# The first layer's last ten chunks by Strassen's scheme too, and the seven products chained in two banks

## Chip, cores and metric

One Trainium2 chip, one core. The metric is the device time of one execution in microseconds (us). Engines: PE is TensorE, DVE is VectorE, ACT is ScalarE, POOL is GpSimd, SP is SyncE, whose queue issues all DMAs of this kernel.

## What is computed

Sliding-window attention (4 batches, 8 heads, 576 positions, head size 64, window 64), then two feed-forward layers over 2304 tokens, each 512 to 2048 to 512, in float32:

```python
attn_out = _attn_ref(q, k, v)                      # softmax over the last 64 positions
x = attn_out.transpose(0, 2, 1, 3).reshape(B * S, H * D)     # 2304 x 512
h = x @ w_in;  g = h * np.clip(h + 3.0, 0.0, 6.0) / 6.0;  x = g @ w_out
h = x @ w2_in; g = np.maximum(0.01 * h, h);               out = g @ w2_out
```

## The kernel before

Every float32 operand of the layers is split into a rounded high half and a low half, and each product is three matmuls: high by high, low by high, high by low. `rounded` and `halves` make the halves of 128 x 512 pieces of the weights, on ScalarE and VectorE; the pieces lie in rings of 7 tiles each (`w0h`, `w0l` for the layer's first weights, `w1h`, `w1l` for its second).

**Plain chunks.** In the first layer a chunk is 128 of the 2048 hidden features. For a block of tokens (four of 512 and one of 256) `st_h` makes 12 matmuls into a PSUM bank `h`; ScalarE and VectorE turn that into the halves `gh` and `gl`; `st_y` makes 12 matmuls into the banks `y0` to `y3`. The 16 chunks go in groups of 6, 5 and 5; a group runs over all blocks before the next begins, and its sums go to `xb` in SBUF (copied for the first group, added by VectorE for the later ones). The attention of block b+1 is spread over block b of the first group; its output `xa0` to `xa4` stays in SBUF for all three groups, and is split into `xs0h` to `xs3l` anew in each.

**Quads.** The second layer works by Strassen's scheme (in Winograd's form). A quad is two chunks in one pass of 768 tokens, and a pass has 8 quads, with 3 passes. Inputs and weights are cut in two by two parts, so that 7 products M1 to M7 of 6 matmuls with 384 columns each (line 848) stand for what would be 8. `inputs` makes the seven input operands of a pass (B11, B21, B22 and the differences T1 to T4). A quad's 11 weight pieces come from `convert_quad`, which makes them on ScalarE and VectorE and stores them to DRAM (`kept`), or from `fetch`, which loads them from there. Four quads are converted ahead, during the first layer (`STAGED`), the other four in the first pass. The sums of the products, their activation and the split into halves give four values C11, C12, C21, C22; 12 groups of three 512-column matmuls (line 921) then take them into six PSUM banks, and these groups of one quad are put between the products of the next, as many after each product as `FILL` says. PSUM has eight banks: two `h`, four `y`, two `a`. Products add up in a bank where the scheme allows: M2 upon M1, M3 upon M5; the rest is added by VectorE (`plus`, line 334).

**Order.** Nothing is ordered by hand except the chain of PE's operations in the second layer. Each operation is noted with its possible engines, an assumed duration and what it reads and writes; `Order.run` then plans the whole program, and every engine gets its instructions in one fixed order, SP's queue too. An engine takes its instructions in that order, so one that waits holds up all behind it.

Of the kernel before, what the change touches and what calls it, by code (L numbers as in the profile page):

```python
# [223 lines left out]
def swa_relu6_leaky_kernel(ctx: ExitStack, tc: tile.TileContext, q, k, v, w_in, w_out, w2_in, w2_out, out):  # L224
# [24 lines left out]
    GROUPS = (6, 5, 5)  # L249
# [8 lines left out]
    NQUAD = NF // 2  # L258
    STAGED = 4
# [12 lines left out]
    kept = [dr.tile([11 * P, DM], F32, name=f"kept{i}") for i in range(NQUAD)]  # L272
# [12 lines left out]
    xa = [buf(f"xa{b}", [P, NK * n], F32, 1) for b, (_, n) in enumerate(blocks)]  # L285
# [237 lines left out]

    def block_of(tok):
        for b, (o, n) in enumerate(blocks):
            if o <= tok < o + n:
                return b, tok - o

    def st_V(n, po, then=None, pps=()):
# [34 lines left out]
        for js, bb, o in groups:  # L564
# [3 lines left out]
                lambda bb=bb, o=o, m=m: xa[bb]().rearrange("p (c l) -> p c l", c=NK)[:, :, o:o + m * W].rearrange(  # L568
# [13 lines left out]
    assert f0 == NF  # L582
# [87 lines left out]

    WAYS = {
# [3 lines left out]
    SEQ = (("M1", "B11"), ("M6", "T2"), ("M2", "B21"), ("M7", "T3"), ("M5", "T1"), ("M4", "T4"), ("M3", "B22"))  # L675
    FILL = (0, 4, 0, 4, 0, 4, 0)
    stage = []
    turn7 = 0
# [5 lines left out]
    def fetch(kk, i):  # L684
        got = ring_tiles(kk)
        for j, t in enumerate(got):
            load(P * DM * 4, lambda t=t: t().bitcast(F32), kept[i][j * P:(j + 1) * P, :], [t], [("kept", i, j)])
        return got

    def convert_quad(i, kk=None):  # L690

        if kk is None:
            if not stage:
                stage.append(buf("at", [P, 9 * DM], F32R, 1))
            homes = [(None, stage[0], lambda j=j: stage[0]()[:, j * DM:(j + 1) * DM]) for j in range(9)]
            got = [od.slot("stage", None, None, None, 0, homes) for _ in range(11)]
        else:
            got = ring_tiles(kk)

        def keep(j):  # L700
            store(P * DM * 4, kept[i][j * P:(j + 1) * P, :], lambda: got[j]().bitcast(F32), [got[j]], [("kept", i, j)])

        f = 2 * i
        a1, a1f = rounded(w2_in[f * P:(f + 1) * P, :])
# [3 lines left out]
        a2, a2f = rounded(w2_in[(f + 1) * P:(f + 2) * P, :])  # L708
# [4 lines left out]
        def combo(dst, d, x, xr, y, yr, alu):  # L713
            op(tensor_tensor(256, d, x, y, alu), [*xr, *yr], [dst])

        combo((s12, 0), lambda: s12()[:, L], lambda: a2f()[:, L], [a2], lambda: a2f()[:, R], [a2], ALU.add)
        combo((s12, 1), lambda: s12()[:, R], lambda: s12()[:, L], [(s12, 0)], lambda: a1f()[:, L], [a1], ALU.subtract)
        halves(DM, lambda: s12()[:, 0:DM], [(s12, 0), (s12, 1)], got[2], got[3], got[2], got[3])
        keep(2)
        keep(3)  # L720
        combo((s34, 0), lambda: s34()[:, L], lambda: a1f()[:, L], [a1], lambda: a2f()[:, L], [a2], ALU.subtract)
        combo((s34, 1), lambda: s34()[:, R], lambda: a1f()[:, R], [a1], lambda: s12()[:, R], [(s12, 1)], ALU.subtract)
        halves(DM, lambda: s34()[:, 0:DM], [(s34, 0), (s34, 1)], got[4], got[5], got[4], got[5])
# [4 lines left out]
        op([("SP", 0.62, lambda: nc.sync.dma_start(out=kept[i][6 * P:7 * P, :], in_=got[6]().bitcast(F32)))],  # L728
           [(got[6], 0), (got[6], 1)], [("kept", i, 6)])
# [362 lines left out]
```

## Time and profile before

| | |
|---|---|
| median of 3 runs | 860.62 us (859.61 to 861.33) |
| the profiled execution | 861.6 us, span 859.8 us |
| PE busy | 843.4 us, 98% |
| DVE, ACT, POOL busy | 537.7, 456.3, 42.6 us |
| DMA | 139.84 MB, mean 163 GB/s |
| mean granted clock of PE | 0.995 |

The span runs from the first to the last instruction; the execution's own time is 1.8 us more. Ends of matmuls are modelled and matmuls overlap, so PE's pace is read from the distance between starts.

### The profile page before, as it was taken

What the parts mean: (1) busy time and instruction counts of PE and PEld (TensorE: products, weight loads), DVE (VectorE), ACT (ScalarE), POOL (GpSimd) and SP (SyncE); (2) the same over time, 40 slices, a digit from 0 to 9 for tenths busy, and PEclk for the clock granted to TensorE, in tenths of its full rate; (3) what the DMA queues carried; (4) which work ended last, traced back from release to release, by engine and by line L of the source; (5) the groups of instructions that cost most, each with busy time, mean ns of one, the idle gap of its engine ahead of it and who ended that gap; (6) DMA issues with size and microseconds to landing.
All of it is one profiled execution on the core that took longest, in us unless ns stands there. A gap on an engine that the chain in (4) does not pass through costs nothing.

```text
span 859.8 us, 13915 instructions
## 1 busy us (share of the span) xinstructions
PE 843.4 (98%) x5104; PEld 728.6 (85%) x5104; DVE 537.7 (63%) x1169; ACT 456.3 (53%) x1024; POOL 42.6 (5%) x45
## 2 busy tenths in 40 slices
PE   6799999999999999999999999999999999999998
PEld 4578888888988888988888999889999998899996
DVE  5999865343788887889884548888432336322323
ACT  4889977563675555665643436666432235422322
POOL 2222221210000000000000000000000000000000
PEclk9999999999999999999999999999999999999999
DMA  8856552100235442365421746669855565764501
GB/s 286 266 176 205 173 185 58 31 24 1 74 111 188 154 146 89 103 216 172 144 76 56 276 144 237 221 220 313 311 191 189 163 210 182 241 215 164 192 29 73
DMA packets 71907, 139.84 MB, mean 163 GB/s; under 512 B 7328, under 2 KB 15520, under 8 KB 71840
## 3 DMA queue, kind: packets, MB, share of 16 engines
q1 hardware_dynamic: 71840, 138.97, 48.7%
q8 instruction: 40, 0.66, 0.3%
q14 instruction: 27, 0.22, 0.1%
HBM read 111.15 MB, written 27.79 MB: 162 GB/s over the span
## 4 chain that ended last, share of the span: by engine, by line
PE 96%; DMA 1%; ACT 1%; SPq 1%; DVE 1%; issue 0%; POOL 0%; DVEq 0%; ACTq 0%
PE h L598 23%; PE y L644 23%; PE h L848 21%; PE y L921 15%; PE a L921 8%; PE a L493 2%; PE h L545 1%; PE a L518 1%; DMA at<-in_v_dram 1%; PE a L545 1%; SPq L337 1%; ACT at L441 0%; PE h L518 0%; PE y L493 0%; PE a L480 0%
## 5 line engine op out<-in xcount | busy, mean ns | idle before, releaser
L644 PE MATMUL y<-gh,w1h 128*128 128x512 f32 (+1 forms) x320 | 119.0, 372 | 0.0
L644 PE MATMUL y<-gl,w1h 128*128 128x512 f32 (+1 forms) x320 | 118.0, 369 | 0.0
L644 PE MATMUL y<-gh,w1l 128*128 128x512 f32 (+1 forms) x320 | 117.9, 368 | 0.0
L848 PE MATMUL h<-xa,w0l 128*128 128x384 f32 x360 | 107.5, 336 | 0.0
L848 PE MATMUL h<-xa,w0h 128*128 128x384 f32 x360 | 107.3, 336 | 0.0
L334 DVE TENSOR_TENSOR qt<-h,qt 128x384 f32<-128x384 f32 x72 | 40.1, 557 | 94.2 <-PE h L848 93.1
L921 PE MATMUL y<-w1h,at 128*128 128x512 f32 x288 | 97.2, 391 | 0.0
L617 ACT ACTIVATE r<-h 128x512 f32<-128x512 f32 (+1 forms) x80 | 44.4, 554 | 98.0 <-PE h L598 97.7
L622 DVE SCALAR_TENSOR_TENSOR r<-r,h 128x512 f32<-128x512 f32 (+1 forms) x80 | 50.6, 632 | 62.4 <-ACT r L617 62.1
L644 PEld LDWEIGHTS y<-gl,w1h 128*128 128x128 f32 x320 | 60.3, 189 | 10.5 <-DVE gl L626 0.4
L644 PEld LDWEIGHTS y<-gh,w1h 128*128 128x128 f32 x320 | 60.3, 189 | 10.1 <-issue 0.3
L644 PEld LDWEIGHTS y<-gh,w1l 128*128 128x128 f32 x320 | 60.4, 189 | 9.6
L848 PEld LDWEIGHTS h<-xa,w0l 128*128 128x128 f32 x360 | 66.5, 188 | 1.8
L848 PEld LDWEIGHTS h<-xa,w0h 128*128 128x128 f32 x360 | 66.4, 188 | 1.8
L825 ACT ACTIVATE qt<-qt 128x384 f32<-128x384 f32 x48 | 25.2, 525 | 74.4 <-DVE qt L334 74.4
L921 PEld LDWEIGHTS y<-w1h,at 128*128 128x128 f32 x288 | 54.1, 188 | 10.6
L626 DVE SCALAR_TENSOR_TENSOR gl<-r,gh 128x512 fp32r<-128x512 f32 (+1 forms) x80 | 51.6, 645 | 14.1 <-ACT gh L319 13.3
L319 ACT ACTIVATE gh<-r 128x512 fp32r<-128x512 f32 (+2 forms) x84 | 48.9, 582 | 17.1 <-DVE r L622 16.8
L357 DVE TENSOR_SCALAR ca<-ca 128x512 uint32<-128x512 uint32 (+1 forms) x128 | 54.5, 434 | 4.8 <-ACT ca L368 4.5
L921 PE MATMUL y<-w1l,at 128*128 128x512 f32 x144 | 56.7, 394 | 0.0
L921 PE MATMUL a<-w1h,at 128*128 128x512 f32 x144 | 50.6, 392 | 0.0
L368 ACT ACTIVATE ca<-st 128x512 f32<-128x512 f32 x64 | 42.5, 669 | 12.5 <-DVE w0l L329 4.0
(206 smaller groups left out, 1828.5 us busy)
## 6 DMA issues: line engine op xcount, KB each, us to landing
w0h<-kept SPq DMA_DIRECT2D x70, 256.0 KB, 3.1
w0l<-kept SPq DMA_DIRECT2D x70, 256.0 KB, 3.1
st<-in_moe_w_in_dram SPq DMA_DIRECT2D x32, 512.0 KB, 3.8
st<-in_moe_w_out_dram SPq DMA_DIRECT2D x32, 512.0 KB, 3.9
kept<-at SPq DMA_DIRECT2D x44, 256.0 KB, 2.3
w1h<-kept SPq DMA_DIRECT2D x40, 256.0 KB, 4.0
w1l<-kept SPq DMA_DIRECT2D x40, 256.0 KB, 4.3
at<-in_v_dram SPq DMA_DIRECT2D x16, 256.0 KB, 3.8
```

Source lines behind the costliest of these rows:

```text
L319: a = act(n, lambda: nc.scalar.activation(out=dst(), in_=src(), func=AF.Copy, scale=scale))
L334: return [dve(n, lambda: nc.vector.tensor_tensor(out=dst(), in0=a(), in1=b(), op=alu))]
L357: return dve(DM, lambda: nc.vector.tensor_scalar(out=dst(), in0=src(), scalar1=s1, scalar2=s2, op0=op0, **({"op1": op1} if op1 else {})), ...
L368: act(DM, lambda: nc.scalar.activation(out=af(), in_=high().bitcast(F32), func=AF.Abs)),
L598: nc.tensor.matmul(ph()[:, 0:n], wt()[:, cs], xt()[:, 0:n], start=(c == 0 and m == 0), stop=(c == NK - 1 and m == 2),)
L617: act(n, lambda: nc.scalar.activation(out=rr(), in_=h(), func=AF.Relu, bias=3.0)),
L622: op([dve(n, lambda: nc.vector.scalar_tensor_tensor(out=rr(), in0=rr(), scalar=6.0, in1=h(), op0=ALU.min, op1=ALU.mult))], [r, ph], [r])
L626: op([dve(n, lambda: nc.vector.scalar_tensor_tensor(out=gl()[:, 0:n], in0=rr(), scalar=1.0 / 6.0, in1=gg().bitcast(F32), op0=ALU.mult, op1 ...
L644: nc.tensor.matmul(y()[:, 0:n], stat()[:, cs], mov()[:, 0:n], start=(first and m == 0), stop=(last and m == 2))
L825: act(HT, lambda: nc.scalar.activation(out=r(), in_=r(), func=AF.Prelu, alpha=0.01)),
L848: nc.tensor.matmul(bk()[:, 0:HT], a, b_(), start=(start and j == 0 and q_ == 0), stop=(j == 1 and q_ == 2), skip_group_check=True,)
L921: nc.tensor.matmul(y(), a()[:, cs], b_(), start=(first and m == 0), stop=(last and m == 2))
```

## The change

The first layer keeps its plain way for the first group of 6 chunks alone. The other ten become five quads, in the same three passes of 768 tokens as the second layer (`QUADS` is 5 and 8). Since the attention output no longer stays in SBUF (`xa` is now a ring of two), `st_h` stores it to DRAM (`xd`), and `inputs` loads the four parts of a pass from there. The first layer's quads have their own activation (`swish`), and their outputs (`outputs0`) go as before into `y0` to `y3` with 512 tokens, and into the two `a` banks with the other 256, to be added to `xb` at a pass's end.

Weights: three of the five quads are converted in the plain part, through the tiles `e0` to `e2`; the other two in the first pass. Four quads of the second layer are converted in the first layer's second and third passes (`AHEAD`), through four tiles of 512 columns (`gh`, `gh`, `gl`, `gl`).

Products, in both layers: the order is now M1, M2, M6, M5, M7, M4, M3. M1, M6, M7 and M4 add up in one `h` bank (`up`), which is copied out to SBUF after M1, M6 and M7; M2 and then M5 with M3 use the other (`side`), and three additions by VectorE join the two. Output groups stand after M6, M7 and, in the first layer, M3.

```diff
-    GROUPS = (6, 5, 5)
+    GROUPS = (6,)
...
-    NQUAD = NF // 2
-    STAGED = 4
+    PLAIN = sum(GROUPS)
+    QUADS = ((NF - PLAIN) // 2, NF // 2)
+    STAGED = (3, 4)
...
-    kept = [dr.tile([11 * P, DM], F32, name=f"kept{i}") for i in range(NQUAD)]
+    xd = dr.tile([P, NK * NT], F32, name="xd").rearrange("p (c l) -> p c l", c=NK)
+    kept = [[dr.tile([11 * P, DM], F32, name=f"kept{j}_{i}") for i in range(n)] for j, n in enumerate(QUADS)]
...
-    xa = [buf(f"xa{b}", [P, NK * n], F32, 1) for b, (_, n) in enumerate(blocks)]
+    xa = [buf("xa", [P, NK * 512]) for _ in blocks]
...
+            store(P * NK * n * 4, xd[:, :, o:o + n], lambda: xblock(b), names, [("xd", b)])
...
-    SEQ = (("M1", "B11"), ("M6", "T2"), ("M2", "B21"), ("M7", "T3"), ("M5", "T1"), ("M4", "T4"), ("M3", "B22"))
-    FILL = (0, 4, 0, 4, 0, 4, 0)
+    SEQ = (("M1", "B11"), ("M2", "B21"), ("M6", "T2"), ("M5", "T1"), ("M7", "T3"), ("M4", "T4"), ("M3", "B22"))
+    FILL = ((0, 0, 8, 0, 4, 0, 4), (0, 0, 6, 0, 6, 0, 0))
+    AHEAD = [(p, i) for p in (1, 2) for i in (0, 2)]
...
-    def convert_quad(i, kk=None):
+    def stage_homes(layer):
...
+            if layer == 0:
+                tiles_ = [buf(f"e{m}", [P, 4 * HT], F32R, 1) for m in range(3)]
+                stage[0] = [(None, t, lambda t=t, j=j: t()[:, j * DM:(j + 1) * DM]) for t in tiles_ for j in range(3)]
+            else:
+                tiles_ = [buf(g, [P, DM], F32R) for g in ("gh", "gh", "gl", "gl")]
+                stage[1] = [(None, t, lambda t=t: t()[:, 0:DM]) for t in tiles_]
+        return stage[layer]
...
+    def convert_quad(layer, i, kk=None):
...
-            if not stage:
-                stage.append(buf("at", [P, 9 * DM], F32R, 1))
-            homes = [(None, stage[0], lambda j=j: stage[0]()[:, j * DM:(j + 1) * DM]) for j in range(9)]
-            got = [od.slot("stage", None, None, None, 0, homes) for _ in range(11)]
+            got = [od.slot(("stage", layer), None, None, None, 0, stage_homes(layer)) for _ in range(11)]
         else:
             got = ring_tiles(kk)
...
-        s12 = buf("kt", [P, 768])
-        s34 = buf("kt", [P, 768])
+        s = buf("st", [P, DM, 2], U32, bufs=3)
...
-    def second_layer():
+    def paired():
...
+        for x, tag in (("B11", "xa"), ("B21", "xa"), ("T2", "e0"), ("T1", "e1"), ("T3", "e2")):
...
+        t = buf("wx", [P, HT], F32, 1)
+        whomes += [(None, t, lambda t=t: t()[:, 0:HT])]
+        gslots = [((grid, j), lambda j=j: grid()[:, j * HT:(j + 1) * HT]) for j in range(12)]
...
+        def inputs(layer, p):
...
+                if layer:
+                    names = [("y1", b, c) for b in over for c in (2 * kh, 2 * kh + 1)]
+                    src[x] = names, lambda: xb[:, 2 * kh:2 * kh + 2, o:o + HT]
+                else:
+                    t = buf("st", [P, DM, 2], U32, bufs=3)
...
+                    load(P * 2 * HT * 4, view, xd[:, 2 * kh:2 * kh + 2, o:o + HT], [t], [("xd", b) for b in over])
...
+        def swish(r, hi, lo):
+            a = work()
+            op([
+                act(HT, lambda: nc.scalar.activation(out=a(), in_=r(), func=AF.Relu, bias=3.0)),
...
+            op([dve(HT, lambda: nc.vector.scalar_tensor_tensor(
+                out=r(), in0=a(), scalar=6.0, in1=r(), op0=ALU.min, op1=ALU.mult
+            ))], [r, a], [r])
+            op(copy(HT, hi[1], r, True, 1.0 / 6.0), [r], [hi[0]])
+            op([dve(HT, lambda: nc.vector.scalar_tensor_tensor(
+                out=lo[1](), in0=r(), scalar=1.0 / 6.0, in1=hi[1]().bitcast(F32), op0=ALU.mult, op1=ALU.subtract
+            ))], [r, hi[0]], [lo[0]])
+
...
+            value = leaky if layer else swish
+            up, side = bank("h", 2), bank("h", 2)
             for pos, (m, x) in enumerate(SEQ):
-                name = {"M1": "X", "M2": "X", "M6": "Y", "M7": "Y", "M4": "Y", "M5": "V", "M3": "V"}[m]
-                if name not in banks2:
-                    banks2[name] = bank("h", 2)
-                bk = banks2[name]
-                product(m, x, bk, m not in ("M2", "M3"))
+                product(m, x, side if m in ("M2", "M5", "M3") else up, m in ("M1", "M2", "M5"))
                 if m == "M1":
-                    wk["s"] = ring("wk", whomes)
-                    op(copy(HT, wk["s"], lambda bk=bk: bk()[:, 0:HT]), [bk], [wk["s"]])
+                    r11 = out_of(up)
+                elif m == "M2":
+                    plus(r11, side)
+                    value(r11, *slots["C11"])
                 elif m == "M6":
-                    plus(wk["s"], bk, wk["s"])
-                elif m == "M2":
-                    g["C11"] = value(ring("wk", whomes), bk)
+                    r12 = out_of(up)
                 elif m == "M7":
-                    wk["u"] = ring("wk", whomes)
-                    plus(wk["u"], bk, wk["s"])
-                elif m == "M5":
-                    r = ring("wk", whomes)
-                    plus(r, bk, wk["u"])
-                    g["C22"] = value(r)
+                    r22 = out_of(up)
+                    plus(r22, side)
+                    value(r22, *slots["C22"])
                 elif m == "M4":
-                    plus(wk["u"], bk, wk["u"])
-                    g["C21"] = value(wk["u"])
-                else:
-                    plus(wk["s"], bk, wk["s"])
-                    g["C12"] = value(wk["s"])
-                for _ in range(FILL[pos]):
+                    if layer:
+                        leaky(work(), *slots["C21"], up)
+                    else:
+                        swish(out_of(up), *slots["C21"])
+                elif m == "M3":
+                    plus(r12, side)
+                    value(r12, *slots["C12"])
+                for _ in range(plan[pos]):
...
-        def values_out(p, i, wt, g):
+        def outputs0(p, i, wt, g):
...
+                def fn():
+                    for m, (a, b_) in enumerate(((hi, gh), (lo, gh), (hi, gl))):
+                        nc.tensor.matmul(
+                            y()[:, d:d + n], a()[:, cs], b_[1]()[:, t0:t0 + n], start=(begins and m == 0),
+                            stop=(last and m1 and m == 2), skip_group_check=(n < 512),
+                        )
...
+            for k, f in enumerate((1, 0)):
+                for n in (512, 256):
+                    for c in range(NK):
+                        todo.append(lambda n=n, f=f, c=c, k=k: part(n, f, c, k == 0, k == 1))
...
+        def outputs1(p, i, wt, g):
...
-            order = [("C11", 0, 0), ("C22", 1, 1), ("C21", 1, 0), ("C12", 0, 1)]
+            order = (("C21", 1, 0), ("C22", 1, 1), ("C11", 0, 0), ("C12", 0, 1))
...
-                                op(copy(DM, z, y), [y], [z])
+                                t = buf("st", [P, DM, 2], U32, bufs=3)
+
                             else:
-                                z = buf(f"xs{c}{'hl'[half]}", [P, DM], F32, 1)
-                                for k in range(2):
-                                    ks = slice(k * 256, (k + 1) * 256)
-                                    src, dst = (lambda ks=ks: y()[:, ks]), (lambda ks=ks: z()[:, ks])
-                                    op([copy(256, dst, src)[k]], [y], [(z, k)])
-                            zs = [z] if p < NPAIR - 1 else [(z, 0), (z, 1)]
+                                t = z = buf(f"xs{c}{'hl'[half]}", [P, DM], F32, 1)
+                            op(copy(DM, z, y), [y], [t])
...
+        for layer in range(2):
+            for p in range(NPAIR):
+                inputs(layer, p)
+                for i in range(QUADS[layer]):
+                    if p == 0 and i >= STAGED[layer]:
+                        wt = convert_quad(layer, i, kk)
+                    else:
+                        wt = fetch(layer, i, kk)
+                    if not layer and (p, i) in AHEAD:
+                        convert_quad(1, AHEAD.index((p, i)))
...
+                    quad(layer, wt, slots, todo, plan)
+                    todo, plan = (outputs1 if layer else outputs0)(p, i, wt, g), FILL[layer]
...
-                if f == GROUPS[0] + GROUPS[1]:
-                    for i in range(STAGED // 2):
-                        convert_quad(i)
                 convert(f)
-                if f == NF - 1:
-                    for i in range(STAGED // 2, STAGED):
-                        convert_quad(i)
+                if f == PLAIN - 1:
+                    for i in range(STAGED[0]):
+                        convert_quad(0, i)
...
-    second_layer()
+    paired()
```

PE, a quad of the first half of the second layer before: M1 (into `h_5823`), then M6 (into `h_5835`), then the first output group. Names are tiles, with the planner's numbers.

```order
L848 MATMUL h_5823<-xa0_4437,w0h_5587 128x384
L848 MATMUL h_5823<-xa0_4437,w0l_5598 128x384
L848 MATMUL h_5823<-xa0_4437,w0h_5587 128x384 x2
L848 MATMUL h_5823<-xa0_4437,w0l_5598 128x384
L848 MATMUL h_5823<-xa0_4437,w0h_5587 128x384
L848 MATMUL h_5835<-xa1_4744,w0h_5626 128x384
L848 MATMUL h_5835<-xa1_4744,w0l_5644 128x384
L848 MATMUL h_5835<-xa1_4744,w0h_5626 128x384 x2
L848 MATMUL h_5835<-xa1_4744,w0l_5644 128x384
L848 MATMUL h_5835<-xa1_4744,w0h_5626 128x384
L921 MATMUL y0_5432<-w1h_5353,at_5369 128x512
```

PE, the start of a first-layer quad in the change: M1 (into `up`, here `h_3392`), M2 (into `side`, `h_3403`), and M6's first matmul.

```order
L887 MATMUL h_3392<-xa_2684,w0h_3152 128x384
L887 MATMUL h_3392<-xa_2684,w0l_3156 128x384
L887 MATMUL h_3392<-xa_2684,w0h_3152 128x384 x2
L887 MATMUL h_3392<-xa_2684,w0l_3156 128x384
L887 MATMUL h_3392<-xa_2684,w0h_3152 128x384
L887 MATMUL h_3403<-xa_2845,w0h_3152 128x384
L887 MATMUL h_3403<-xa_2845,w0l_3156 128x384
L887 MATMUL h_3403<-xa_2845,w0h_3152 128x384 x2
L887 MATMUL h_3403<-xa_2845,w0l_3156 128x384
L887 MATMUL h_3403<-xa_2845,w0h_3152 128x384
L887 MATMUL h_3392<-e0_2786,w0h_3174 128x384
```

M6 has moved from a bank of its own into the bank that M1 has just filled, with one product between the two.

SP, before: DMA issues beside the first layer's later chunks, when quads of the second layer are staged. `st` are weights as they come, `at` holds the staged pieces.

```order
L337 DMA st<-in_moe_w_in_dram 128x1024
L341 DMA kept_70<-at 128x512 x5
L728 DMA kept_70<-at 128x512
L337 DMA st<-in_moe_w_out_dram 128x1024
L341 DMA kept_70<-at 128x512 x2
L337 DMA st<-in_moe_w_in_dram 128x1024
```

SP, in the change: the first layer's second pass. `kept_2_72` and `kept_3_73` are first-layer quads 2 and 3, `kept_0_75` the second layer's quad 0.

```order
L339 DMA w1l<-kept_2_72 128x512
L339 DMA w1h<-kept_3_73 128x512
L339 DMA w0h<-kept_3_73 128x512
L339 DMA w0l<-kept_3_73 128x512
L339 DMA w1l<-kept_3_73 128x512
L343 DMA kept_0_75<-gh 128x512 x2
L339 DMA st<-in_moe_w_out_dram 128x1024 x2
L339 DMA w0h<-kept_3_73 128x512
L339 DMA w0l<-kept_3_73 128x512
L343 DMA kept_0_75<-gl 128x512
L343 DMA kept_0_75<-gh 128x512
```

Where the queue held weights to be converted and stores of staged pieces, it now also holds the fetches that PE needs for its next quads.

## Rows read from the trace of the kernel before

**Rows 1.** The page, busy time of the engines over the whole span.

```profile
PE 843.4 (98%) x5104; PEld 728.6 (85%) x5104; DVE 537.7 (63%) x1169; ACT 456.3 (53%) x1024; POOL 42.6 (5%) x45
```

**Rows 2.** Windows: length, busy us of PE, PEld, DVE, ACT, POOL, clock, DMA.

```profile
0.00:20.00 20.00, 12.60 (x138) 9.19 (x142) 10.26 (x30) 9.36 (x28) 5.12 (x13) 0.96 0.88 282
20.00:40.00 20.00, 15.40 (x225) 11.84 (x217) 17.47 (x40) 16.83 (x41) 5.73 (x5) 0.87 0.85 281
40.00:60.00 20.00, 19.47 (x183) 14.84 (x182) 19.69 (x43) 17.78 (x62) 5.84 (x5) 1.00 0.59 188
240.00:260.00 20.00, 20.00 (x90) 16.57 (x89) 18.31 (x33) 13.29 (x25) 0.00 (x0) 1.00 0.35 123
520.00:540.00 20.00, 20.00 (x101) 17.96 (x100) 17.22 (x37) 12.62 (x25) 0.00 (x0) 1.00 0.58 207
580.00:600.00 20.00, 20.00 (x103) 18.27 (x102) 17.73 (x31) 12.88 (x25) 0.00 (x0) 1.00 0.91 302
600.00:620.00 20.00, 20.00 (x102) 18.05 (x101) 11.07 (x20) 10.12 (x21) 0.00 (x0) 1.00 0.93 324
```

**Rows 3.** The chain that ended last, one quad: start, length, what.

```profile
784.08 3.14 PE h L848 x18
787.22 2.76 PE y L921 x12
789.98 2.10 PE h L848 x12
...
799.72 3.14 PE h L848 x18
```

**Rows 4.** Timeline of PE, first layer, from 512-token to 256-token block: start, length.

```profile
343.56 0.39 PE L644 MATMUL y<-gh,w1h 128*128 128x512 f32 x1
...
344.24 0.28 PE L598 MATMUL h<-xs0h,w0h 128*128 128x256 f32 x1
...
346.75 0.28 PE L598 MATMUL h<-xs0h,w0h 128*128 128x256 f32 x1
```

**Rows 5.** Timeline of all engines around M3, M1 and M6, second layer.

```profile
722.24 0.34 PE L848 MATMUL h<-xs3l,w0l 128*128 128x384 f32 x1
...
722.62 0.56 DVE L334 TENSOR_TENSOR qt<-h,qt 128x384 f32<-128x384 f32 x1 [0.53 <-PE h L848]
...
723.29 0.51 PE L848 MATMUL h<-xa,w0h 128*128 128x384 f32 x2
...
723.66 0.49 ACT L319 ACTIVATE r<-h 128x384 f32<-128x384 f32 x1 [0.69 <-PE h L848]
```

**Rows 6.** Groups by line and shape: count, busy us, mean ns, idle before.

```profile
L329 DVE CUSTOM_DVE_ANT_0 ca<-ca,cr 128x1024 uint16<-128x1024 uint16 x64 | 46.1, 722 | 0.2
L373 DVE SCALAR_TENSOR_TENSOR ca<-st,ca 128x512 uint32<-128x512 uint32 x64 | 45.0, 706 | 0.4
L626 DVE SCALAR_TENSOR_TENSOR gl<-r,gh 128x512 fp32r<-128x512 f32 x64 | 44.9, 702 | 13.0 <-ACT gh L319 12.2
...
L334 DVE TENSOR_TENSOR qt<-h,qt 128x384 f32<-128x384 f32 x72 | 40.1, 557 | 94.2 <-PE h L848 93.1 <-ACT ca L368 0.7
L357 DVE TENSOR_SCALAR ca<-ca 128x512 f32<-128x512 f32 x64 | 27.9, 436 | 4.5 <-ACT ca L368 4.5
...
L660 DVE TENSOR_TENSOR xb<-y,xb 128x512 f32<-128x512 f32 x32 | 21.0, 684 | 3.1 <-PE y L644 3.1
...
L626 DVE SCALAR_TENSOR_TENSOR gl<-r,gh 128x256 fp32r<-128x256 f32 x16 | 6.7, 420 | 1.2 <-ACT gh L319 1.1
...
L329 DVE TENSOR_TENSOR kt<-xb,kt 128x768 f32<-128x768 f32 x6 | 5.7, 953 | 0.1
...
L368 ACT ACTIVATE ca<-st 128x512 f32<-128x512 f32 x64 | 42.5, 669 | 12.5 <-DVE w0l L329 4.0 <-DVE w1l L329 3.1 <-DVE at L329 2.7
...
L825 ACT ACTIVATE qt<-qt 128x384 f32<-128x384 f32 x48 | 25.2, 525 | 74.4 <-DVE qt L334 74.4
...
L319 ACT ACTIVATE qt<-h 128x384 f32<-128x384 f32 x16 | 7.8, 490 | 2.3 <-PE h L848 2.3
```

More of the change, by code (lines that the diff above doesn't have):

```diff
@@ L522, in st_P, with xblock @@
             pts[n].append(pt)
+    def xblock(b):
+        n = blocks[b][1]
+        return xa[b]()[:, 0:NK * n].rearrange("p (c l) -> p c l", c=NK)
     def block_of(tok):
@@ L890, in quad, with part, add @@
                 fill.pop(0)()
-            return g
-        def fetched(wt):
-            return wt[6].whole
         ybanks = {}
-        todo = []
-        def values_out(p, i, wt, g):
+        def outputs0(p, i, wt, g):
+            o = 2 * p * HT
             if i == 0:
+                ybanks.clear()
+                for c in range(NK):
+                    ybanks[c] = bank(f"y{c}")
+                for c in range(0, NK, 2):
+                    ybanks["a", c] = ybanks["a", c + 1] = bank("a", 2)
+            yb = dict(ybanks)
+            first, last = i == 0, i == QUADS[0] - 1
+            todo = []
+            def part(n, f, c, m0, m1):
+                hi, lo = wt[7 + 2 * f], wt[8 + 2 * f]
+                (gh, gl), y = g[f], yb[c] if n == 512 else yb["a", c]
+                d = 0 if n == 512 else (c % 2) * 256
+                t0 = 0 if n == 512 else 512
+                cs = slice(c * P, (c + 1) * P)
+                begins = first and m0 and (n == 512 or c % 2 == 0)
+                def fn():
[4 more added lines that the diff above has]
+                        )
+                op([pe(3 * (0.0132 + n / 2400), fn)], [hi, lo, *gh[0], *gl[0]], [y], chain=True)
+                if last and m1 and (n == 512 or c % 2):
+                    over = [b for b, (s, m) in enumerate(blocks) if s < o + 512 and o < s + m] if n == 512 else \
+                        [b for b, (s, m) in enumerate(blocks) if s < o + 768 and o + 512 < s + m]
+                    cc = (c,) if n == 512 else (c - 1, c)
+                    def add():
+                        if n == 512:
+                            dst, got = xb[:, c, o:o + 512], y()
+                        else:
+                            dst = xb[:, c - 1:c + 1, o + 512:o + 768]
+                            got = y().rearrange("p (c l) -> p c l", c=2)
+                        nc.vector.tensor_tensor(out=dst, in0=got, in1=dst, op=ALU.add)
+                    op([dve(512, add)], [y], [("y1", b, k) for b in over for k in cc])
+            for k, f in enumerate((1, 0)):
+                for n in (512, 256):
+                    for c in range(NK):
+                        todo.append(lambda n=n, f=f, c=c, k=k: part(n, f, c, k == 0, k == 1))
+            return todo
@@ L939, in go @@
+                            op(copy(DM, z, y), [y], [t])
+                            op([("SP", 0.8, lambda: nc.sync.dma_start(out=out[r0:r0 + P, :], in_=z()))], [t],
                                delay=2.0)
[L940 removed]
+                            op([("DMA", P * DM * 4 / 3.6e5, lambda: None)], [t], delay=2.0)
                     todo.append(go)
[L944 to L956 removed]
+            return todo
```

179 lines of the change are left out of this document (98 added, 81 removed).

## The prediction

> **What bounds the kernel now.** I read the page's busy line first, then busy time by stretches, then the chain, then single rows. The busy line gives TensorE (PE) 98% of the span and VectorE (DVE) 63% [rows 1]; a 98% made of pipelined matmuls could still hide waits, so the stretches come next. The first two are the only ones with gaps that matter: PE is busy 12.60 and 15.40 of 20 us, 12.0 us idle, while q, k and v arrive and the softmax runs. Afterwards every stretch shown has PE at 20.00 of 20 and the granted clock at 1.00, whether VectorE is at 18.31 (conversions beside the first layer) or the DMA engines at 0.93 [rows 2]. The chain shows what a saturated PE delivers: a second-layer quad runs from 784.08 to 799.72, 15.64 us, and nothing else stands in it [rows 3]. So time after the start is matmuls times their spacing, and a change is worth what it takes off that sum, less any wait that it opens.
>
> **The spacing.** Three 512-column matmuls of layer one start 0.68 us apart, 0.2267 each, and 21 of 256 columns take 2.51 us, 0.1195 each [rows 4]. In the quad, twelve 512-column ones take 2.76 us, 0.230 each; that leaves (15.64 - 36 x 0.230) / 42 = 0.1752 us for one of 384 columns [rows 3]. At the granted 1.00, the 2.4 GHz level, 512 columns would be 0.2133 us, so each matmul costs about 13 ns beyond its columns, and cutting work into more, shorter matmuls gives part of a saving back. The Trainium skill (TensorE: Matmul & The Clock Gate, Back-to-back issue gap) puts that extra at 2.5 ns; by it the saving below would be 240 x (4 x 0.2158 + 0.1092) - 15 x (42 x 0.1625 + 24 x 0.2158 + 24 x 0.1092) = 14.0 us. The trace does not agree, and the sum goes by the rows.
>
> **What is removed and added on PE.** A plain chunk has 24 matmuls (12 into h, 12 out to y) for each of four blocks of 512 tokens and one of 256: 24 x (4 x 0.2267 + 0.1195) = 24.63 us; ten chunks, 246.3 us. A first-layer quad of the change has 7 products x 6 matmuls of 384 columns and, for two chunks, 24 matmuls of 512 and 24 of 256 into y: 42 x 0.1752 + 24 x 0.2267 + 24 x 0.1195 = 15.67 us; five quads in three passes, 235.0 us. **Gain 11.3 us.** If its 512-column matmuls run at the second layer's 0.230 instead, 236.2 us and a gain of 10.1. The second layer keeps all its matmuls; there I count no gain, since no wait was there to remove.
>
> **Edits costed at nothing, and their cover.** *VectorE.* 50 of 80 chunk steps go, and a first-layer quad brings eight scalar_tensor_tensor of 384 columns (not in the trace; between 0.420 at 256 and 0.702 at 512, I take the middle, 0.561) and three sums at 0.557: 6.2 us. A converted quad is four weight loads of 0.436 + 0.436 + 0.706 + 0.722 and a low half of 0.684 (the fourth without it), four sums at about 0.420 and low halves of 0.684 + 0.684 + 0.420: 14.7 us. New inputs are nine operations of 768 columns at 0.953 and four of 384 at 0.557: 10.8; six sums into xb, 4.1 [rows 6]. A pass has five quads and two conversions: 30.8 + 29.4 + 10.8 + 4.1 = 75.1 us in 78.4 us of PE. The cover is thin, but VectorE at 18.31 of 20 held nothing up [rows 2]. *ScalarE* gets twelve operations of 0.490 to 0.525 a quad, 6.2 us [rows 6], and has the room. *Storing and loading the inputs* (4.7 MB once, then 1.57 MB a pass) and the three quads staged early lie beside the plain chunks, where the DMA share was 0.59 before 60 us and 0.35 at 240 us [rows 2]. If that cover went, a first quad would wait for its inputs, once, for a few us. The start and the tail I leave as they are.
>
> **The sums chained in two banks.** Before, M6 had a bank of its own and M2, the next into M1's bank, stood behind four output groups. Now M6 adds into `up`, so ScalarE must have copied M1's result out while M2 runs. The row for that copy: M1's last matmul starts at 723.29 (the x2 there is this one and M6's first, 0.17 later), the copy starts at 723.66 and takes 0.49, so it is out at 724.15. Six matmuls of M2 in between would put M6 at 723.46 + 6 x 0.1752 = 724.51: 0.36 us to spare, if ScalarE is free [rows 5]. A second-layer quad has two more such places: M4's result must leave `up` during M3, and the sum with M3's must leave `side` during the next M1 (in the first layer four output groups lie between as well). The last is what the trace already has: M3's last matmul starts at 722.24, the sum runs from 722.62 to 723.18, and M6, which needs that bank, starts at 723.46 without a gap, 0.28 later [rows 5]. An operation of 0.5 to 0.67 us that ScalarE has just begun [rows 6] eats this margin and misses it by up to 0.3. What queues behind a late copy is M6, and on ScalarE the activation of C11, which nobody needs for several us. Bounds for the wait per place: 0 (the old place of this kind) and 0.3. With 24 x 3 + 15 x 1 = 87 places I take 1.5 us in all, near the row that shows none; this also stands for the first quads, which have few output groups to put between products.
>
> **DMA.** From the code, a fetched quad is 11 pieces of 256 KB, 2.88 MB, and a converted one 2.10 MB of weights read and 2.88 MB written. Passes two and three of the first layer take ten fetches, four conversions ahead for layer two and two sets of inputs: 28.8 + 19.9 + 3.1 = 51.9 MB in 156.7 us, 331 GB/s. The trace reached 302 and 324 GB/s in neighbouring stretches, at shares of 0.91 and 0.93, that is 332 and 348 at a full share [rows 2]. So these 157 us would run at 95 to 100% of what the rows show, where the old kernel did so for 40. Fetches have slack, because a weight tile of the ring of 14 is refilled for the quad after next. The staged pieces have less: layer two's eleven pass through four tiles (gh, gh, gl, gl), so each write to one waits until its last store has landed, on ScalarE's and VectorE's own queues, with the sums of the products behind it. I take no wait here, since the sum still fits.
>
> **Sum.** Span 859.8 - 11.3 + 1.5 = 850.0. The profiled execution took 861.6 with its 859.8, so it would be 851.8; the median of the runs lies 1.0 below the profiled one, and 860.6 - 11.3 + 1.5 = **850.8 us**.
>
> **Rivals.** *The DMA engines become the bound in passes two and three.* At the stretch's 324 GB/s 51.9 MB take 160.2 us, 3.5 late; at 302, 171.9, 15.2 late; at their mean, 165.8, 9.1 late. That gives 852.8 to 864.5, with 860.6 - 11.3 + 9.1 = 858.4 likeliest. For it: the sum above, the four stage tiles, SyncE's one queue. Against: the ring's slack, and PE at 20.00 beside the share of 0.93. The Trainium skill (DMA: Bandwidth & Descriptors, Bandwidth) speaks for it: it asks for 1 MiB or more a transfer and has 341 GB/s there and 138 at 64 KB, and these are of 256 KB. The trace does not bear that out so far, with 324 GB/s in such pieces.
>
> *The short places cost more than the matmuls save.* It decides at 11.3 / 87 = 0.13 us a place. If ScalarE, with conversions in its queue, is on average 0.2 us late at each, 17.4 us go: 866.7, slower than before. For it: the copy must find ScalarE free within about a third of a microsecond. Against: the old place of this kind, with 0.28 to spare, shows no gap.
>
> *VectorE becomes the bound in the first layer's passes.* If it can give no more than the 18.31 of 20 seen [rows 2], 75.1 us of work take 82.0, 3.6 late in each of three passes: 860.2, no change. Against: durations overlap a little, so 75.1 is an upper figure.
>
> **How the numbers follow.** Forecast (waits of 0 to 4 us) 0.70, its own range 847.5 to 853.5: from the gain of 11.3 and none, with 2 us for the start, to 10.1 and 3. DMA 0.14, half of it within 1.7 us of the old time or above; short places 0.08; VectorE 0.04; a shifted start or something unseen 0.04. A measurement here tells 0.2%, 1.7 us, from no change. Faster: 0.70 + 0.07 + 0.02 + 0.02 = 0.81. The same: 0.08. Slower: 0.11, from the short places and the upper half of the DMA case. The range runs from 847.5 to 859.0, the middle of the DMA case, and leaves out some 0.2.
>
> **What would show it.** If the steps are right, the changed profile has first-layer quads 15.6 to 15.8 us apart from about 232 us on, PE at 20.00 of 20 in every stretch after 60 us, DMA shares of 0.9 and more from 310 to 470 us, and no wait of PE of over 1 us behind an ScalarE copy. Quads of 16.5 us in passes two and three with VectorE or ScalarE idle behind a store of `kept` would be the DMA rival; gaps of some 0.1 to 0.3 us before M6 or before M1 in quad after quad, with all else in time, the short places. I would be wrong outright if the stretch before 60 us grew, since nothing here prices it.

## The result, and the profile after

The changed kernel takes **851.64 us** (median of four, 850.54 to 852.34) against 860.74 beside it: a ratio of 0.9895, 95% interval 0.9878 to 0.9912, faster by 7.6 to 10.5 us. Forecast were 850.8 us, in a range of 847.5 to 859.0. The profiled execution took 850.54 us with a span of 848.5, the fastest of the four; the other three had spans of 849.4 to 850.2.

The page's busy line answers to [rows 1]: PE is at 98% as before, with 12.4 us less busy time in 150 more matmuls, and ScalarE has 506.0 us where it had 456.3.

```profile
PE 831.0 (98%) x5254; PEld 740.1 (87%) x5254; DVE 543.6 (64%) x1184; ACT 506.0 (60%) x1146; POOL 43.0 (5%) x45
```

The windows answer to [rows 2]: length, busy us of PE, PEld, DVE, ACT and POOL, clock, DMA share and GB/s. The fifth row is passes two and three of the first layer.

```profile
0.00:20.00 20.00, 13.87 (x145) 10.06 (x145) 10.24 (x30) 9.86 (x28) 5.12 (x13) 1.00 0.91 298
20.00:40.00 20.00, 13.95 (x213) 10.81 (x212) 18.97 (x42) 17.72 (x48) 5.47 (x5) 0.96 0.87 292
40.00:60.00 20.00, 19.63 (x155) 15.10 (x153) 19.20 (x41) 17.34 (x54) 2.96 (x3) 0.95 0.64 212
60.00:80.00 20.00, 19.39 (x239) 15.85 (x240) 18.38 (x52) 17.49 (x54) 6.43 (x5) 1.00 0.73 233
320.63:477.63 157.00, 157.00 (x903) 146.80 (x901) 131.26 (x251) 98.90 (x195) 0.00 (x0) 1.00 0.90 322
```

Gaps of PE stand in the start alone, now with 0.61 us between 60 and 80 us. In passes two and three PE is busy 157.00 of 157.00 us, and this is where the DMA rival, and with pass one the VectorE rival, would have had to show: DMA at 322 GB/s and a share of 0.90, VectorE at 131.26, that is 65.6 us a pass. The short places lie in the second layer too, where PE has no gap either.

The chain that ended last answers to [rows 3]; here is a quad of the first layer: start, length, what.

```profile
305.09 3.12 PE h L887 x18
308.22 2.76 PE y L958 x12
310.98 1.43 PE a L958 x12
312.41 2.08 PE h L887 x12
314.50 2.76 PE y L958 x12
317.26 2.10 PE h L887 x12
319.36 1.43 PE a L958 x12
320.79 3.12 PE h L887 x18
```

From 305.09 to 320.79 there is nothing but matmuls: **15.70 us**, and all 13 distances from the first layer's third quad to the second layer's first are 15.70. The second layer, in the same view:

```profile
730.09 2.76 PE y L1010 x12
732.85 1.36 PE a L1010 x6
734.21 2.10 PE h L887 x12
736.32 2.76 PE y L1010 x12
739.08 1.36 PE a L1010 x6
```

Output groups stand in two places there, and quads follow each other every **15.57 us**, not every 15.64.

If each matmul is charged with the time from its start to the next one's, the two traces differ by part like this (us):

| part | before | after | difference | forecast |
|---|---|---|---|---|
| attention and its gaps | 75.37 | 75.83 | +0.46 | 0 |
| first six chunks | 155.99 | 156.36 | +0.37 | 0 |
| ten chunks, now five quads in three passes | 246.57 | 235.57 | -11.00 | -11.3, and +1.5 of waits in both layers |
| second layer | 375.44 | 373.87 | -1.57 | 0 |
| from PE's end to the end of the span | 3.92 | 4.28 | +0.36 | 0 |
| span, with what lies ahead of the first matmul | 859.8 | 848.5 | -11.3 | -9.8 |

The two profiles lie 11.3 us apart and the medians 9.1, since the start differs from one execution to the next: three profiles of the changed kernel reach the first Strassen product at 232.24, 232.74 and 233.76 us and need 616.2 to 616.8 from there to the end; the first is the one shown. The kernel before varies likewise, from 857.8 to 864.7 us in all its runs.

### The profile page after: what moved, and what is told of

The parts are those of the page before. It is cut to its first block, busy times and chain, and to the rows that moved or that the text cites. A ratio compares the mean times of both kernels' runs of the same rounds, so it can differ in the third digit from the quotient of the medians.

```text
span 848.5 us, 14680 instructions
## 1 busy us (share of the span) xinstructions
PE 831.0 (98%) x5254; PEld 740.1 (87%) x5254; DVE 543.6 (64%) x1184; ACT 506.0 (60%) x1146; POOL 43.0 (5%) x45
## 4 chain that ended last, share of the span: by engine, by line
PE 93%; DVE 3%; ACT 1%; DMA 1%; SPq 1%; issue 0%; ACTq 0%; DVEq 0%
PE h L887 34%; PE y L1010 16%; PE y L958 10%; PE h L604 8%; PE y L650 8%; PE a L1010 8%; PE a L958 5%; PE a L495 1%; PE h L551 1%; DMA at<-in_v_dram 1%; PE a L520 1%; ACT at L443 1%; SPq L339 1%; PE a L551 1%; DVE nb L454 1%; DVE ca L331 0%
## 5 line engine op out<-in xcount | busy, mean ns | idle before, releaser
L887 PE MATMUL h<-e,w0h 128*128 128x384 f32 x354 | 105.7, 335 | 0.0
L887 PE MATMUL h<-e,w0l 128*128 128x384 f32 x348 | 104.5, 335 | 0.0
L321 ACT ACTIVATE qt<-h 128x384 f32<-128x384 f32 x77 | 37.6, 488 | 73.7 <-PE h L887 73.5
L958 PE MATMUL y<-at,w1h 128*128 128x512 f32 x240 | 79.4, 391 | 0.0
L887 PEld LDWEIGHTS h<-e,w0h 128*128 128x128 f32 x354 | 65.4, 188 | 0.9
L887 PEld LDWEIGHTS h<-e,w0l 128*128 128x128 f32 x348 | 64.4, 188 | 0.9
L359 DVE TENSOR_SCALAR ca<-ca 128x512 f32<-128x512 f32 (+1 forms) x128 | 57.0, 451 | 7.3 <-ACT ca L370 6.4
L958 PE MATMUL a<-at,w1h 128*128 128x256 f32 x240 | 47.8, 282 | 0.0
L958 PE MATMUL y<-at,w1l 128*128 128x512 f32 x120 | 47.2, 394 | 0.0
L331 DVE CUSTOM_DVE_ANT_0 ca<-ca,cr 128x1024 uint16<-128x1024 uint16 x64 | 46.5, 731 | 0.9
L375 DVE SCALAR_TENSOR_TENSOR ca<-st,ca 128x512 uint32<-128x512 uint32 x64 | 45.6, 719 | 0.5
```

Of the source, the lines that this page charges most:

```text
L321: a = act(n, lambda: nc.scalar.activation(out=dst(), in_=src(), func=AF.Copy, scale=scale))
L331: d = dve(n, lambda: nc.vector.tensor_tensor(out=dst(), in0=a(), in1=b(), op=alu))
L359: return dve(DM, lambda: nc.vector.tensor_scalar(out=dst(), in0=src(), scalar1=s1, scalar2=s2, op0=op0, **({"op1": op1} if op1 else {})), ...
L375: op([dve(DM, lambda: nc.vector.scalar_tensor_tensor(out=a(), in0=high(), scalar=0xC0000000, in1=a(), op0=ALU.bitwise_and, op1=ALU.bitwise ...
L887: nc.tensor.matmul(bk()[:, 0:HT], a, b_(), start=(start and j == 0 and q_ == 0), stop=(j == 1 and q_ == 2), skip_group_check=True,)
L958: nc.tensor.matmul(y()[:, d:d + n], a()[:, cs], b_[1]()[:, t0:t0 + n], start=(begins and m == 0), stop=(last and m1 and m == 2), skip_grou ...
```

## The experiments

All ratios are against the kernel before, run on the same chip; they need not be the quotient of two medians. The medians of two rows can come from different chips.

| run | median us | ratio, interval |
|---|---|---|
| old_two_fills | 861.16 | 1.0001, 0.9982 to 1.0021 |
| one_fill | 850.04 | 0.9878, 0.9863 to 0.9892 |
| six_quads | 857.61 | 0.9972, 0.9956 to 0.9989 |
| copy_twice | 864.95 | 1.0031, 1.0008 to 1.0054 |
| more_loads | 872.81 | 1.0132, 1.0103 to 1.0162 |
| more_vector | 854.01 | 0.9914, 0.9885 to 0.9943 |
| late_vector | 865.86 | 1.0052, 1.0031 to 1.0073 |
| free_loads | 857.21 | 0.9947, 0.9930 to 0.9965 |
| fewer_places | 851.59 | 0.9888, 0.9865 to 0.9911 |
| changed_again | 851.52 | 0.9867, 0.9841 to 0.9894 |
| changed_third | 851.72 | 0.9895, 0.9881 to 0.9910 |
| one_fill_tail | 849.25 | 0.9869, 0.9848 to 0.9889 |

**Where the second layer's 1.57 us come from: old_two_fills and one_fill.** The first edits the kernel before and leaves its three banks and its order of products alone; the second edits the changed kernel.

```diff
-    FILL = (0, 4, 0, 4, 0, 4, 0)
+    FILL = (0, 6, 0, 6, 0, 0, 0)
```

> The kernel before, with only the places of its output groups in a second-layer quad changed: six after M6 and six after M7 in place of four after each of M6, M7 and M4; same order of products, same three banks, same matmuls. Theory (a change of output length on TensorE costs about 0.035 us, and a quad of the second layer of the changed kernel is 0.07 us shorter because it has two such places in place of three): quads fall from 15.64 to 15.57 us, 23 of them 1.6 us less, median 859.1. Rival (the two-bank chaining shortens the quads of the second layer): they stay at 15.64 us and the time at 860.7.

```diff
-    FILL = ((0, 0, 8, 0, 4, 0, 4), (0, 0, 6, 0, 6, 0, 0))
+    FILL = ((0, 0, 8, 0, 4, 0, 4), (0, 0, 0, 0, 12, 0, 0))
```

> The changed kernel, with the twelve output groups of a second-layer quad in one place, after M7, in place of six after M6 and six after M7. Theory of the length changes: second-layer quads of 15.50 us in place of 15.57, 1.6 us less in 23 quads, 850.0 if the changed kernel is at 851.6. Rival (short places: M6 to M7 then has only M5 between, as M2 to M5 has only M6): a wait there of 0.1 to 0.3 us a quad, quads of 15.6 to 15.8 us, 852.5 to 857. By the slack of 0.35 us that the places between M1 and M6 have in the changed kernel, no wait is expected.

In old_two_fills, quads fall from 15.64 to 15.58 us, with the old chaining; so the two banks are not what shortens them. Its median did not move, and in its profile one quad takes the gain back: at the turn to the second pass it takes 17.24 us, PE waiting for ScalarE's copies of the finished sums, which wait for the output before in the same tile. In one_fill the chain shows one place and quads of 15.51 to 15.54 us (one of 15.82):

```profile
726.41 7.31 PE h L887 x42
733.72 2.76 PE y L1010 x12
736.48 1.36 PE a L1010 x6
737.84 2.72 PE y L1010 x12
740.56 1.36 PE a L1010 x6
741.92 3.14 PE h L887 x18
```

The rows show the reason: the same twelve 512-column matmuls take 2.76 us behind 384-column ones (733.72), and 2.72 (737.84) where 512-column ones came before. In the kernel before, the quad of [rows 3] has three places, the first at 787.22 and the others here:

```profile
792.09 1.39 PE a L921 x6
793.48 1.37 PE y L921 x6
...
796.96 1.39 PE y L921 x6
798.35 1.37 PE a L921 x6
```

Matmul by matmul, on average over the second layer of the changed kernel, the first nine of 512 columns behind a change start 229, 233, 236, 224, 231, 236, 228, 233 and 231 ns apart, then 226 to 227; together 41 ns more than 9 x 226.7; the first seven of 384 behind a change start 171 to 185 apart, together 26 more than 7 x 173.3. That is 67 ns for a place, there and back. It accounts for the 15.64, 15.57 and 15.51 to 15.54 us of three places, two and one, and for the 0.230 us that the prediction read from [rows 3]. The change of bank is not the cost: in the last ten plain chunks of the kernel before, PE goes between `h` and `y` at one length, and 512 columns keep 0.227 us on average.

**The short places: copy_twice.**

```diff
                 if m == "M1":
                     r11 = out_of(up)
+                    op([copy(HT, r11, lambda: up()[:, 0:HT])[0]], [up], [r11])
```

> The changed kernel, in which ScalarE copies M1's result out of its bank twice, one copy right behind the other, so that M6 has to wait for the second too; the output stays the same. In the changed kernel that copy ends 0.35 us before M6 starts, in every one of the 39 quads, and a copy takes 0.49. Theory (the place has 0.35 us of slack and nothing else is in its way): M6 waits about 0.14 us in every quad, 39 x 0.14 = 5.5 us more, some 857. Rival (a wait at this place is absorbed, since weights are loaded ahead and the next products move up): no measurable change. Rival (ScalarE's other work collides with the longer pair): 0.3 us a quad and more, 863 or slower.

All quads but the first two grew by 0.35 us and a little more (to 16.05 and 15.92), and the median is 13.3 us above the changed kernel's. Two timelines show how, first the changed kernel, then copy_twice: ScalarE's copy of M1, M2's last matmul, M6's first and second.

```profile
728.05 0.49 ACT L321 ACTIVATE wx<-h 128x384 f32<-128x384 f32 x1
...
728.72 0.33 PE L887 MATMUL h<-xa,w0h 128*128 128x384 f32 x1
...
728.89 0.33 PE L887 MATMUL h<-e,w0h 128*128 128x384 f32 x1
```

```profile
739.76 1.01 ACT L321 ACTIVATE wx<-h 128x384 f32<-128x384 f32 x2
...
740.42 0.34 PE L887 MATMUL h<-xa,w0h 128*128 128x384 f32 x1
...
740.82 0.44 PE L887 MATMUL h<-e,w0h 128*128 128x384 f32 x1
...
741.10 0.34 PE L887 MATMUL h<-e,w0l 128*128 128x384 f32 x1
```

In the changed kernel the copy ends at 728.54, 0.35 before M6 at 728.89; the prediction had 0.36. With two copies it ends at 740.77, and M6, due 0.17 behind 740.42, starts at 740.82 and not at 740.59: 0.23 late, of which 0.05 is from the copy's end to PE's start. The next matmul then follows 0.28 later, not 0.17. So a late copy costs its lateness, here 0.18 us, and some 0.16 besides: 0.05 from its end to PE's start and 0.11 ahead of the next matmul, which my expectation of 0.14 left out. The time is that of the second rival, but no other work of ScalarE stands between: both copies together take 1.01 us. The place was free because the copy came in time, not because lateness is absorbed.

**VectorE's cover: more_vector and late_vector.** Both add six additions of 224 columns a first-layer quad: more_vector on a tile alone, late_vector's reading that quad's values. Both edits, in this order:

```diff
+                if not layer and m != "M1":
+                    t = spare
+                    op(vector_only(224, t, t, t, ALU.add), [t], [t])
...
+                if not layer and m in ("M2", "M7", "M4"):
+                    for k, v in slots[{"M2": "C11", "M7": "C22", "M4": "C21"}[m]]:
+                        op(vector_only(224, spare, lambda v=v: v()[:, 0:224].bitcast(F32), spare, ALU.add), [k, spare], [spare])
```

> The changed kernel with six more additions of 224 columns on VectorE in each first-layer quad, on a tile that nothing else uses: some 0.38 us each, 2.3 us a quad, 11.5 us a pass, so that VectorE has about 77 of a pass's 78.5 us where the changed kernel has 65.6. Theory of the prediction's rival (VectorE gives at most 18.31 of 20 us, 71.9 a pass): TensorE waits some 5 us a pass, 15 us in all, 867. If VectorE's cover is good to the full pass: quads stay at 15.70 us and the time at 851.6.

> As more_vector, but each of the six additions of a first-layer quad reads one of that quad's own activated values, so that none can run ahead of it: some 0.39 us each, 2.3 us a quad, 11.7 us a pass, VectorE at about 77 of 78.5 us where the changed kernel has 65.6. If VectorE gives at most 18.31 of 20 us: some 5 us a pass of waiting, 15 us in all, 867. If its cover is good to the full pass: 851.6 to 853, quads of 15.70 us with at most a few longer ones.

more_vector tells nothing of the question: its additions depend on no product, the planner put them early, and the last ran at 303 us. late_vector's stand where they belong, 90 of 0.386 us, 11.6 a pass. Nearly all quads still take 15.70 us, but one takes 26.51, at the turn to the third pass, and the second layer's second 17.11. Windows at the first, columns as above:

```profile
386.00:391.00 5.00, 3.00 (x20) 2.36 (x18) 4.67 (x9) 3.96 (x9) 0.00 (x0) 1.00 1.03 356
391.00:395.00 4.00, 2.26 (x6) 1.44 (x6) 4.00 (x8) 1.84 (x5) 0.00 (x0) 0.74 0.79 292
395.00:399.00 4.00, 1.48 (x4) 0.96 (x4) 4.00 (x7) 2.50 (x4) 0.00 (x0) 0.50 0.74 242
399.00:403.00 4.00, 4.00 (x12) 3.33 (x12) 4.00 (x9) 2.16 (x5) 0.00 (x0) 0.50 0.76 247
403.00:407.00 4.00, 4.00 (x26) 3.81 (x25) 2.83 (x8) 0.93 (x2) 0.00 (x0) 0.98 0.26 101
```

VectorE is busy 4.00 of 4 while PE waits for the new pass's inputs, whose sums and low halves stand behind it. PE's granted clock then falls to 0.50, the 1.2 GHz level, and stays there until 403: with PE busy 4.00 of 4 again, 384-column matmuls start 0.32 us apart, not 0.17. The rival's 15 us were right in size (865.86 for 867 expected), but not in their place: 10.8 us come at this turn, 1.5 at the start of the second layer, and the rest ahead of the first Strassen product. VectorE is not held to 18.31 of 20 either; what counts is the cover at the turn of a pass, not its mean.

**The DMA engines' margin: more_loads and free_loads.** Both copy four more pieces a fetched quad to DRAM that nothing reads; free_loads, shown here, gives each piece an area of its own, where more_loads has `spare[j - 7]` for all quads and no wait for `wt[0]`.

```diff
                         wt = fetch(layer, i, kk)
+                        if not layer and p:
+                            for j in range(7, 11):
+                                op([("SP", 0.62, lambda p=p, i=i, j=j: nc.sync.dma_start(
+                                    out=spare[(p - 1) * 5 + i][(j - 7) * P:(j - 6) * P, :],
+                                    in_=kept[0][i][j * P:(j + 1) * P, :]))],
+                                   [("kept", 0, i, j), wt[0]], [("spare", p, i, j)])
```

> The changed kernel with four more pieces of 256 KB moved for each fetched quad in passes two and three of the first layer, from the stored weights to a DRAM area that nothing reads: 40 pieces, 10.5 MB read and written again, in 157 us in which the changed kernel moves 322 GB/s at a share of 0.90. Theory of the prediction's rival (the DMA engines are within a few per cent of the bound there): the share goes to 1.0, quads of these passes grow past 15.70 us, and the time is 7 to 17 us longer, 859 to 869. If the fetches have more slack than that: quads stay at 15.70 us, 851.6, and the share is still near 1.0.

> As more_loads, with a DRAM area of its own for each of the 40 pieces, so that no piece waits for another into the same area, and each issued only with its quad. If more_loads stood still because its pieces waited for one another, quads stay near 15.70 us and the time at 851.6 to 854, with the DMA share near 1.0. If the DMA engines are the bound once these 10.5 MB are added: the share at 1.0 through passes two and three, quads above 15.70 in many places, 859 to 872.

more_loads lost 22.6 us in two quads at the start of pass two (25.11 and 28.92 us), because its pieces waited for each other in SyncE's one queue; this row of the waits, 290 to 400 us, has the total, the count and the longest:

```profile
SPq L1051 <- DMA spare<-kept: 21.6, 8, 5.5
```

So it shows what a stuck queue costs, not where the engines' bound is. free_loads comes nearer to that: six quads of 15.83 to 17.81 us, 7.3 us more in the profile, no long stop. Its windows:

```profile
340.00:360.00 20.00, 20.00 (x116) 18.47 (x116) 17.82 (x37) 12.49 (x25) 0.00 (x0) 1.00 1.03 389
360.00:380.00 20.00, 17.80 (x102) 16.25 (x101) 12.27 (x24) 10.09 (x21) 0.00 (x0) 1.00 1.01 366
380.00:400.00 20.00, 18.68 (x101) 16.03 (x100) 14.04 (x23) 10.64 (x21) 0.00 (x0) 1.00 1.03 386
...
321.52:486.40 164.88, 160.56 (x906) 147.09 (x905) 133.32 (x255) 99.12 (x196) 0.00 (x0) 1.00 0.97 352
```

Over these passes the changed kernel moves 322 GB/s without a wait, free_loads 352 with 7.3 us of them, so the average can rise by at most some 9% here. It is an average that is meant: the changed kernel, too, reaches 390 GB/s at a share of 1.04 from 360 to 380 us, with PE at 20.00 of 20. In free_loads the share stays at 1 for longer, a piece of stored weights takes 5.7 us to land where the changed kernel has 5.1 (medians in these passes), and the chain that ended last goes, around PE's waits, through loads and stores of 5.3 to 7.4 us.

**How far the saving goes on: six_quads.**

```diff
-    GROUPS = (6,)
+    GROUPS = (4,)
```

> The changed kernel with four plain chunks and six Strassen quads in the first layer in place of six and five. Theory of the sum (two chunks of 24.63 us against three quads of 15.70): 2.2 us less than the changed kernel, about 849.4. Rival (the plain chunks are the cover of the attention stage): the first 182 us then hold some 164 us of VectorE and 160 us of ScalarE work, TensorE waits for the softmax, and the time is 851.6 or more, with the stretch up to the first Strassen product longer than 182 us and gaps of TensorE after 65 us.

The quads keep their 15.70 us (one takes 16.85), but the first starts at 190.95 us where 180 would be two chunks earlier (232.24 - 2 x 26.06, a sixth of the 156.36 us of the first six chunks). Windows of the start:

```profile
0.00:20.00 20.00, 10.76 (x132) 8.00 (x136) 10.45 (x30) 9.45 (x28) 5.13 (x13) 0.89 0.89 282
20.00:40.00 20.00, 14.67 (x229) 11.01 (x221) 17.30 (x39) 16.32 (x45) 5.20 (x5) 0.93 0.79 256
40.00:60.00 20.00, 16.35 (x186) 11.30 (x185) 18.83 (x41) 16.54 (x56) 5.84 (x5) 0.93 0.72 243
60.00:80.00 20.00, 18.95 (x185) 15.11 (x186) 18.09 (x58) 18.73 (x63) 4.17 (x4) 1.00 0.64 212
```

Over the first 80 us PE is busy 60.73 us, where the changed kernel has 66.84. The plain chunks are what PE does while the softmax runs; with four of them the start gives back more than the 2.2 us gained.

**A shorter version: fewer_places and one_fill_tail.** fewer_places merges the output groups in both layers and splits the last six output copies; one_fill_tail has the first layer's `(0, 0, 8, 0, 4, 0, 4)` back. Each ran beside the changed kernel.

```diff
-    FILL = ((0, 0, 8, 0, 4, 0, 4), (0, 0, 6, 0, 6, 0, 0))
+    FILL = ((0, 0, 8, 0, 8, 0, 0), (0, 0, 0, 0, 12, 0, 0))
...
-                            op(copy(DM, z, y), [y], [t])
...
+                                ts_ = [(t, 0), (t, 1)]
+                                for k in range(2):
+                                    ks = slice(k * 256, (k + 1) * 256)
+                                    op([copy(256, lambda ks=ks: z()[:, ks], lambda ks=ks: y()[:, ks])[k]],
+                                       [y], [ts_[k]])
```

> The changed kernel itself once more, for its time beside the next one on the same chip. By the sum of the matmuls: 849 to 852, quads of 15.70 and 15.57 us as in its profile; where two executions differ, the difference lies ahead of the first Strassen product.

> The changed kernel with its output groups in fewer places (first layer eight after M6 and eight after M7, second layer all twelve after M7), and with the last six copies of the output split between ScalarE and VectorE as in the kernel before. Theory of the length changes and the tail: 1.5 us less in the second layer (15.51 for 15.57 us), 0.3 in the first (15.68 for 15.70), 0.4 at the end, 2.2 us less than the changed kernel run beside it. Rival (a chip that does not show it, since executions differ by 2 us at the start): within 0.2% of the changed kernel.

fewer_places did not beat the changed kernel (851.59 beside 851.52). The second layer has its 15.51 to 15.54 us, but five first-layer quads and the second layer's first take 15.93 to 17.37, some 4.9 us more in the profiled execution, the slowest of six. The chain at the longest:

```profile
412.11 6.87 DMA st<-in_moe_w_out_dram
418.98 0.02 issue
419.00 0.66 ACT ca L370
419.66 0.39 ACT qt L321
420.05 0.04 issue
420.10 3.54 PE h L887 x18
```

A weight load lands late, ScalarE stands in order at the conversion that needs it, M4's copy is behind that, and M1 of the next quad, with only M3 in between, starts 1.5 us late. One more of the six waits at M1; two wait at M6 for M1's copy, a place that the changed kernel has as well, and one at M2 for an input. In the changed kernel four output groups after M3 cover this place: 1.77 us from the end of the copy to M1 in the median of 15 quads, against 0.35 in the second layer, where conversions stand in the first pass alone.

> The changed kernel itself, for its time beside the next one on the same chip: 849 to 852, quads of 15.70 and 15.57 us.

> The changed kernel with its first layer as it is, the second layer's twelve output groups in one place after M7, and the last six copies of the output split between ScalarE and VectorE. Theory of the length changes and the tail: second-layer quads of 15.52 us in place of 15.57 (23 of them: 1.2 us less), 0.4 us less between TensorE's end and the end of the span, no wait in the first layer, so 1.6 us less than the changed kernel beside it, about 849.9. Rival (the first layer's waits in fewer_places came from the second layer's plan or from the split tail, and not from its own): first-layer quads of 16 us and more return, 855.

one_fill_tail takes 849.25 us, the changed kernel beside it 851.72: 2.5 us less, the lowest median of all. The intervals of the two overlap, and executions of changed_again reached 848.14, so the size of the gain is not shown. Of the 1.8 us between the two profiles 0.8 lie behind the first Strassen product and 1.0 ahead of it, where executions differ anyway. Its first layer is back at 15.70 (one quad of 16.31), its second at 15.51 to 15.54 (one of 15.81), and 3.83 us lie between PE's end and the span's, near the 3.92 before the change. The split copies are not what shortens the tail: one_fill, which has none, needs 3.65 us there. In both, the last output lands 2.1 us after its issue and not 2.7 as in the changed kernel; why it does stays open.

## Why the prediction was right, point by point

- **The matmul sum.** Right: 11.0 us for 11.3. A quad takes 15.70 for 15.67: its 512-column matmuls run at 0.2301 us on average, the layer-two spacing that I had put at the lower end, and those of 384 and 256 columns at 0.1744 and 0.1191, a little under the rows.
- **The second layer.** "There I count no gain, since no wait was there to remove" missed 1.57 us. I had both spacings, 0.2267 and 0.230, and took them for properties of the layers; old_two_fills and one_fill show that they go by the changes of length, of which the change takes one place out of three. The prediction left this term at nothing without asking why the two spacings differ.
- **The short places.** 1.5 us were counted; the profile shows none, and two more profiles 0.3 and 0.5, each at M6 of one quad. The 0.36 us to spare was right to 0.01. The rival charged a late copy with its lateness alone (0.2 us at 87 places, 17.4 us); copy_twice shows some 0.16 us more for each.
- **DMA.** 331 GB/s forecast, 322 at 0.90 measured, the share on average only: from 400 to 410 us it is 0.64. Not the bound, but the margin is some 9% at most. The Trainium skill (DMA: Bandwidth & Descriptors, Bandwidth) asks for 1 MiB a transfer and has 341 GB/s there. The trace differs: free_loads moved 389 GB/s over 20 us, mostly in pieces of 256 KB.
- **VectorE.** 65.6 us a pass for at most 75.1. The count was near, since the durations add up to 73.7 a pass, and they overlap, as the rival's "against" said. late_vector's 77 broke the cover, at the turn of a pass.
- **Start and tail.** Left as they were. The stretch up to the first Strassen product grew by 0.83 us in the profiles shown, less than it varies by itself. The sign of being wrong, a longer stretch before 60 us, did not come there: PE is busy 47.45 us in it, 47.47 before (46.15 in changed_again). "Every stretch shown" at 20.00 of 20 was a misreading: [rows 2] has 19.47 from 40 to 60 us. The tail grew by 0.36, and by as much in two more profiles.

Against the forecast span of 850.0 the profiled one, 848.5, is 1.5 us short for waits that did not come and 1.6 for the second layer, and 1.5 long at start, tail and spacing. That the last balances one of the first two is luck; the 11 us in the ten chunks are not. The median came out 0.8 us above its forecast, and not 1.5 below, since the profiled execution before was 1.0 us above its median and this one is 1.1 below.

## What to carry to other kernels

Where a saturated engine sets the time, count its instructions at spacings from the trace, and when one kind has two spacings, look at what stands ahead of it before calling either one its price. A slack read between two engines says whether a place is free, not what it costs when it is missed; adding the suspected work tells that, and it must depend on its place, or the scheduler moves it away. Work that fills the wait at the start is part of the price of replacing it.

## What the runs showed of the hardware

- A change of output length between 384 and 512 columns cost TensorE 67 ns there and back, spread over the next sixteen matmuls.
- A matmul that had to wait was followed by the next 0.28 us later, not 0.17 (copy_twice). In late_vector the granted clock was 0.50 from 395 to 403 us, behind stretches with PE busy 3.00 of 5 and 2.26 of 4 us, so a wait cost more than its own length.
- The DMA share read 1.03 at 389 GB/s and 1.01 at 366 (free_loads), so a share near 1.0 is no fixed rate.
